# Layer B, one core: sums, values, inverses and scalings of two halves issued apart, filling in smaller pieces, inverse totals on Pool

## The chip, the cores and the metric

The kernel runs on 1 core of one Trainium2 chip. The metric is the device time of one execution in microseconds (us). A core has five engines that run their own instruction streams and wait for one another through semaphores: PE (matrix multiply; its weight loads are listed apart as PEld), DVE (vector), ACT (scalar), POOL (GpSimd) and SP, which issues DMA. In the timelines below, the work of an engine runs in the order in which the program issues it to that engine (the KT copy at 1005.63 us comes after the multiply at 1005.22, as issued), so what stands ahead of an instruction on its engine is part of its cost.

## The reference, cut to what matters

The model is four layers, A, B, A, B. Only B is changed. B walks through 2048 tokens in 64 segments of 32. Each segment is joined to 8 memory rows, and the first 8 output rows are the memory of the next segment, so the segments are serial.

```python
for s in range(n_seg):                              # 64 steps
    xs = x[:, s * seg_len:(s + 1) * seg_len, :].copy()
    h = jnp.concatenate([mem, xs], axis=1)          # 8 + 32 rows
    q = jnp.einsum('btd,dhe->bhte', h, Wq)          # 32 heads of 128; k and v alike
    ...
    scores = jnp.where(mask[None, None], scores, -1000000000.0)
    p = _softmax(scores, axis=-1)
    o = jnp.einsum('bhqk,bhke->bhqe', p, v)
    o = jnp.einsum('bhte,hed->btd', o, Wo)
    mem = o[:, :M, :].copy()                        # the next step waits for this
    outs.append(o[:, M:, :])
```

## The kernel before

The 32 heads are worked on as two halves, b = 0 and 1. For a half, `scores(b)` makes the logits and ACT their exponentials (PT). PE then makes the softmax sums (a matrix of ones times PT) and the values (V times PT) into a PSUM buffer pair, `OTL[b, 0]` and `OTL[b, 1]`. ACT makes the inverses R of the sums as exp(-ln(sum)), and DVE multiplies the values by R into OTsb, which the output passes (OPS) read. There are only two OTL buffers: those of half 1 are those of half 0 again, free when DVE's multiplies of half 0 are done. The multiplies and inverses are named (b, jp) below: (0,1) is the second quarter. The other names: QT and KT are queries and keys, transposed for the scores, and TPQ and TPK are PE's transposes that they are copied from; msb is a step's output in bf16, MT its memory rows transposed, hT the next step's input; tsb and ttp are results of the filling and their transposes. `ln_norm` is the layernorm of later tokens, and one of its operations, pow, runs on Pool.

```python
            def sums_and_values(b):
                for jp in range(2):
                    OTL[b, jp] = pot.tile([128, 2, 2, 256], F32, name="b_OTL", tag="ot")   # 2 buffers
                ...  # 8 matmuls of sums, then 32 of values

            def normalize(b, jp):
                R = (wk if general else sm).tile([128, 2, 160], F32, name="b_R", tag="R")   # 2 buffers
                o = OTL[b, jp]
                nc.scalar.activation(out=R[:], in_=o[:, :, 1, 0:160], func=ACT.Ln)
                acc = {} if general else {"accum_out": seen[:, 2 + 2 * b + jp:3 + 2 * b + jp]}
                nc.scalar.activation(out=R[:], in_=R[:], func=ACT.Exp, scale=-1.0, **acc)
                h = 16 * b + 8 * jp
                nc.vector.tensor_tensor(out=OTsb[:, h:h + 8, :]..., in0=o[:, :, 0, 0:160], in1=R[:], op=ALU.mult)
            ...
            if not general:
                sums_and_values(0)
                normalize(0, 0)
            TPKb = transp4(Ksb[:, 1, :], "b_TPK")
            scatter("dve", TPKb, 1, heads(KT[s]), 0, 8, 24)       # KT: the second scores need it
            ...
            scores(1)
            normalize(0, 1)
            for f in vparts[3:]:
                f()
            evac("dve", Vsb[:, 1, :], Vb[:])                      # Vsb: the second values need it
            fill(0.9)
            sums_and_values(1)
            normalize(1, 0)
            normalize(1, 1)
            op = OPass(lambda h: OTsb[:, h, 0:32], HORDER, "b_OPS")
            op.run(8)
            fill(0.7 if i4 else 0.9)
            op.run(8)
            ops = op.ps
            fill(0.4)
            ...      # msb (ACT), MT (PE), hT (DVE and ACT): the memory of the next step
```

`fill` gives PE independent work where it would wait. With i4 the number of the step modulo 4, in three of four steps it is ten parts of four matmuls (b_tail), in the fourth (i4 = 0) sixteen parts of a deferred output pass (b_OPSd). `general` is False on the path that runs. The totals of sums and inverses (`seen`, `C.tot`) only feed a range check at the end.

Of the kernel before, what the change touches and what calls it, by code (L numbers as in the profile page):

```python
# [18 lines left out]
F32 = mybir.dt.float32  # L19
BF16 = mybir.dt.bfloat16  # L20
ACT = mybir.ActivationFunctionType
ALU = mybir.AluOpType
AX = mybir.AxisListType
# [6 lines left out]
NCH = 5  # L30
# [549 lines left out]
def layer_B(nc, tc, C, W, wo_src, x_src, xb_src, x_dst, mem0, general, nsteps=64, out_bf16=False):  # L580
# [8 lines left out]
    nc = _OrdNC(tc, nc_raw, engines=ORDER_ENGINES)  # L589
    assert nsteps % 4 == 0  # L590
    NT = nsteps // 4
    with ExitStack() as ctx:
        st = ctx.enter_context(tc.tile_pool(name="b_state", bufs=1))
        wk2 = ctx.enter_context(tc.tile_pool(name="b_wk2", bufs=2))
        hp = qkp = sm = wk2
        wk = st
# [10 lines left out]
        nc.vector.tensor_tensor(out=selm[:, 1, :], in0=C.identb[:, 56:64], in1=C.identb[:, 120:128], op=ALU.add)  # L607
        ones = st.tile([128, 128], BF16, name="b_ones")
        nc.vector.memset(ones[:], 1.0)
        XO = st.tile([64, 320], F32, name="b_XO")  # L610
        nc.vector.memset(XO[:], 0.0)
        negs = wk.tile([128, 32], F32, name="b_negs", tag="Qsb")
# [64 lines left out]
        hT, QT, KT = {}, {}, {}  # L677

        def heads(t):
            return t[:, 0:1280].rearrange("p (h c) -> p h c", c=40)  # L680
# [36 lines left out]
        def scatter(eng, tp, b, dst3, t0, t1, c0):  # L717
            src = tp[:].rearrange("p i (j t) -> p i j t", j=4)[:, :, :, t0:t1]
            dst = dst3[:, 16 * b:16 * b + 16, c0:c0 + (t1 - t0)].rearrange("p (j i) c -> p i j c", j=4)
            evac(eng, dst, src)  # L720
# [83 lines left out]

        def add_out(ops, XO, name):

            nc.vector.tensor_tensor(out=XO[0:64, :], in0=ops[0:64, :], in1=XO[0:64, :], op=ALU.add)
            if out_bf16:
                xnb = wk.tile([64, 320], BF16, name=name, tag=name)
                nc.vector.tensor_tensor(out=xnb[0:64, :], in0=ops[64:128, :], in1=XO[0:64, :], op=ALU.add)  # L810
                return xnb
# [19 lines left out]
        for kind in ("Q", "K", "V"):  # L831
            for b in range(2):
                u = TailUnit(0, kind, b, ("act", "dve")[b])
# [23 lines left out]
        for s in range(nsteps):  # L857
            last = (s == nsteps - 1)
            T, i4 = divmod(s, 4)
# [8 lines left out]
            if i4 == 0:  # L868
                units = [deferred.pop(T - 1)] if T >= 1 else []
            elif T + 1 < NT:  # L870
                kind = " VQK"[i4]
                units = [TailUnit(T + 1, kind, 0, "act"), TailUnit(T + 1, kind, 1, "dve")]
            else:
                units = []
            queue = [(0.22, u) for u in units for _ in range(NCH)] if i4 else [(0.15, u) for u in units for _ in range(16)]

            def fill(us):

                while queue and us > 0.05:
                    cost, u = queue.pop(0)  # L880
                    u.run(1)
                    us -= cost

            cols = lambda c: hT[s][:, c, 24:56]
# [4 lines left out]
            PT = wk.tile([128, 2, 2, 4, 40], BF16, name="b_PT", tag="PT")  # L889
            OTsb = wk.tile([128, 32, 40], BF16, name="b_OTsb", tag="OTsb")  # L890
            OTL = {}
            if not general:
                seen = sm.tile([128, 6], F32, name="b_seen", tag="seen")
            mrows = []

            def row_max(b):

                negm = wk.tile([128, 16], F32, name="b_negm", tag="negm")
                for q in range(2):
                    sp = ps_tile([40, 8, 40], F32, "b_Sq")  # L900
                    nc.tensor.matmul(sp[:], lhsT=C.identb[:, 0:40], rhs=maskq[:].unsqueeze(1).to_broadcast([128, 8, 40]),
                                     start=True, stop=False, skip_group_check=True)
                    for i in range(8):
                        h = 16 * b + 8 * q + i
                        nc.tensor.matmul(sp[:, i, :], lhsT=QT[s][:, 40 * h:40 * h + 40], rhs=KT[s][:, 40 * h:40 * h + 40],
                                         start=False, stop=True, skip_group_check=True)
                    nc.vector.tensor_reduce(out=negm[0:40, 8 * q:8 * q + 8], in_=sp[:], axis=AX.X, op=ALU.max, negate=True)
                parts = wk.tile([128, 3, 16], BF16, name="b_mparts", tag="mparts")
                for i in range(3):
                    nc.vector.tensor_copy(parts[0:40, i, :], negm[0:40, :])  # L910
                    if i < 2:
                        nc.vector.tensor_tensor(out=negm[0:40, :], in0=negm[0:40, :], in1=parts[0:40, i, :], op=ALU.subtract)
                tp = ps_tile([48, 40], BF16, "b_mt")
                nc.tensor.transpose(tp[:], parts[0:40].rearrange("p i h -> p (i h)"), C.identb[0:40, 0:40])
                ms = wk.tile([48, 40], BF16, name="b_ms", tag="ms")
                nc.vector.tensor_copy(ms[:], tp[:])
                mr = wk.tile([3, 16, 40], BF16, name="b_mrows", tag="mrows")
                for i in range(3):
                    nc_raw.sync.dma_start(mr[i:i + 1, :, :], ms[16 * i:16 * i + 16, :])
                mrows.append(mr)  # L920
# [18 lines left out]
                acc = {} if general else {"accum_out": seen[:, b:b + 1]}  # L939
                nc.scalar.activation(out=PT[:, b], in_=sp[:], func=ACT.Exp, **acc)  # L940

            def sums_and_values(b):

                for jp in range(2):
                    OTL[b, jp] = pot.tile([128, 2, 2, 256], F32, name="b_OTL", tag="ot")
                def ot(j):
                    return OTL[b, j // 2][:, j % 2]
                for k, n in ((0, 32), (1, 8)):
                    for j in range(4):
                        nc.tensor.matmul(ot(j)[:, 1, 0:160], lhsT=ones[32 * j:32 * j + n, :], rhs=PT[32 * j:32 * j + n, b, k].rearrange("p r c -> p (r c)"),  # L950
                                         start=(k == 0), stop=(k == 1), tile_position=(32 * j, 0))
                for r in range(4):
                    for k, n in ((0, 32), (1, 8)):
                        V_ = Vsb if k == 0 else Vt[s]
                        for j in range(4):
                            nc.tensor.matmul(ot(j)[:, 0, 40 * r:40 * r + 40], lhsT=V_[32 * j:32 * j + n, b, 128 * r:128 * r + 128],
                                             rhs=PT[32 * j:32 * j + n, b, k, r, :], start=(k == 0), stop=(k == 1), tile_position=(32 * j, 0))

            def normalize(b, jp):
                R = (wk if general else sm).tile([128, 2, 160], F32, name="b_R", tag="R")  # L960
                o = OTL[b, jp]
                nc.scalar.activation(out=R[:], in_=o[:, :, 1, 0:160], func=ACT.Ln)
                acc = {} if general else {"accum_out": seen[:, 2 + 2 * b + jp:3 + 2 * b + jp]}
                nc.scalar.activation(out=R[:], in_=R[:], func=ACT.Exp, scale=-1.0, **acc)
                h = 16 * b + 8 * jp
                nc.vector.tensor_tensor(out=OTsb[:, h:h + 8, :].rearrange("p (j r) c -> p j (r c)", j=2), in0=o[:, :, 0, 0:160], in1=R[:], op=ALU.mult)

            Qa = thin_mm(cols, W.wq, 0, "b_Qa")
            evac("act", Qsb[:, 0, :], Qa[:], SCB)
# [23 lines left out]
            TPQb = transp4(Qsb[:, 1, :], "b_TPQ")  # L993
            scatter("act", TPQb, 1, heads(QT[s]), 0, 8, 24)
            if not last:
                scatter("act", TPQb, 1, heads(QT[s + 1]), 8, 32, 0)
            if not general:
                sums_and_values(0)
                normalize(0, 0)
            TPKb = transp4(Ksb[:, 1, :], "b_TPK")  # L1000
            scatter("dve", TPKb, 1, heads(KT[s]), 0, 8, 24)
            if not last:
# [4 lines left out]
            if general:  # L1007
                row_max(0)
                scores(0)
                sums_and_values(0)  # L1010
                normalize(0, 0)
                row_max(1)
            scores(1)
            normalize(0, 1)
            for f in vparts[3:]:
                f()
            evac("dve", Vsb[:, 1, :], Vb[:])
            fill(0.9)
            sums_and_values(1)
            normalize(1, 0)  # L1020
            normalize(1, 1)
            op = OPass(lambda h: OTsb[:, h, 0:32], HORDER, "b_OPS")
            op.run(8)
            fill(0.7 if i4 else 0.9)
            op.run(8)
            ops = op.ps
            fill(0.4)
            if not general:
                nc.gpsimd.tensor_tensor(out=C.tot[:, 0, 0:2], in0=C.tot[:, 0, 0:2], in1=seen[:, 0:2], op=ALU.add)
                nc.gpsimd.tensor_tensor(out=C.tot[:, 1, 0:4], in0=C.tot[:, 1, 0:4], in1=seen[:, 2:6], op=ALU.add)  # L1030
            g_need = (s + 6) // 4
            if s % 4 == 2 and g_need < NT:
                ln_norm(g_need)
# [11 lines left out]
            if not last:  # L1045
# [9 lines left out]
                fill(9)  # L1055
                if i4 != 3:
                    tails_to_seg(s + 1)
            for u in units:
                if isinstance(u, TailUnit):
                    u.transposes()  # L1060
                    u.finish()
            if not last and i4 == 3:
                tails_to_seg(s + 1)
            if s % 4 == 1 and (s + 7) // 4 < NT:
# [16 lines left out]
            if last:  # L1081
                od = deferred.pop(T)
                od.run(100)
                store_deferred(T, od)
            hT.pop(s); QT.pop(s); KT.pop(s); Vt.pop(s)


def full_kernel(tc, A_x, A_wq, A_wk, A_wv, A_wo, A_beta, B_x, B_mem0, B_Wq, B_Wk, B_Wv, B_Wo, B_seg_len, out, layers="ABAB"):
# [89 lines left out]
```

## Time and profile before

| | before |
|---|---|
| time, median of 3 runs | 3167.43 us (3160.98 to 3169.33) |
| the 128 steps of layer B, from the trace | about 2,370 us of a span of 3,160 us |
| one step, by its place in a group of four | 17.77, 19.07, 19.46, 17.77 us |

Four successive steps, i4 = 1, 2, 3 and 0, in the table of stretches (start and end in us, length, then per engine busy us and number of instructions, granted PE clock as a share of full speed, DMA share, GB/s):

```profile
996.34:1014.11 17.77, 15.98 (x392) 8.46 (x393) 6.82 (x16) 8.80 (x27) 3.48 (x12) 1.00 0.10 23
1014.11:1033.18 19.07, 16.63 (x400) 8.87 (x400) 8.74 (x21) 9.46 (x28) 2.54 (x8) 1.00 0.06 12
1033.18:1052.64 19.46, 16.88 (x407) 9.01 (x405) 7.01 (x16) 9.98 (x28) 1.13 (x4) 1.00 0.09 21
1052.64:1070.41 17.77, 15.96 (x418) 9.08 (x417) 6.32 (x15) 8.27 (x25) 1.52 (x6) 1.00 0.06 15
```

PE is the busiest and no other engine is busy for more than 52% of a step. PE's waits are then what can be won. This is the view of who waited for whom, PE alone, over the whole run (waiter and its instruction, what it waited for: total us, times, longest us):

```profile
PE b_OTL L86 <- DVE b_OTsb L86: 87.7, 128, 1.2
PE b_SP L86 <- DVE b_KT L86: 78.0, 128, 0.9
PE b_ttp L86 <- DVE b_tsb L86: 37.6, 64, 0.9
PE b_OTL L86 <- DVE b_Vsb L86: 36.3, 128, 0.3
...
PE b_OPS L86 <- DVE b_OTsb L86: 18.5, 93, 0.5
```

The same in order of time, in the timeline of one step (start, length, engine, operation, output<-inputs, count, and in brackets the idle time before it and what ended it):

```profile
1005.22 0.49 DVE L86 TENSOR_TENSOR b_OTsb<-b_OTL,b_R 128x320 bf16<-128x320 f32 x1 [1.31 <-ACT b_R L86]
1005.63 0.48 DVE L86 COPY b_KT<-b_TPK 128x128 bf16<-128x128 bf16 x2
1005.90 0.38 PE L86 MATMUL b_SP<-b_QT,b_KT 128*32 128x40 bf16 x32 [0.53 <-DVE b_KT L86]
...
1006.38 0.44 ACT L86 ACTIVATE b_PT<-b_SP 128x320 bf16<-128x320 f32 x1 [1.25 <-PE b_SP L86]
...
1006.81 0.43 ACT L86 ACTIVATE b_R<-b_OTL 128x320 f32<-128x320 f32 x1
...
1007.87 0.49 DVE L86 TENSOR_TENSOR b_OTsb<-b_OTL,b_R 128x320 bf16<-128x320 f32 x1 [1.76 <-ACT b_R L86]
1008.28 0.68 DVE L86 CAST b_Vsb<-b_V 128x512 bf16<-128x512 f32 x1
1008.42 0.31 PE L86 MATMUL b_OTL<-b_PT,b_ones 32*128 32x160 bf16 x6 [0.64 <-DVE b_OTsb L86]
...
1009.32 1.27 PE L86 MATMUL b_OPS<-b_wo,b_OTsb 128*32 128x320 bf16 x32
1009.48 0.44 ACT L86 ACTIVATE b_R<-b_OTL 128x320 f32<-128x320 f32 x1 [1.64 <-PE b_OTL L86]
```

One reads it from PE backwards. The second sums (1008.42) wait for the multiply that starts at 1007.87; that one waits for the inverse whose Ln (1006.81) ACT runs behind the second PT (1006.38); PT waits for the scores; and the scores (1005.90) wait for a copy that DVE runs behind another multiply (1005.22). It is a zigzag through three engines, none of them full.

The prediction also rests on two groups of Pool additions, for their cost by size (busy us, mean ns):

```profile
L86 POOL TENSOR_TENSOR a_Onat<-a_ts 128x320 bf16<-128x320 f32 x48 | 49.1, 1023 | 11.7 <-DVE a_ts L86 11.7
...
L86 POOL TENSOR_TENSOR c_tot<-c_tot,a_r 128x16 f32<-128x16 f32 x64 | 14.0, 219 | 3.9 <-DVE a_r L86 3.9
```

### The profile page before, as it was taken

To read this page: it belongs to the slowest core of one execution; us is meant where nothing else is said; L and a number is where in the kernel's file an instruction comes from. 1 tells how busy PE (TensorE), PEld (TensorE's weight loads), DVE (VectorE), ACT (ScalarE), POOL (GpSimd) and SP (SyncE) were. 2 spreads that over 40 slices of the span, in tenths; PEclk is the share of its full clock that TensorE was granted. 3 is DMA by queue.
4 is the path that set the end of the run, shared out by engine and by line. 5 is a ranking of instruction groups with operands and counts; after the bars stand their busy time and mean duration, and the time that the engine had idled before them with its cause. 6 is when DMAs were issued, how large, how long until landed. Compare 5 with 4: busy or idle time off the path is not lost.

```text
span 3160.3 us, 128983 instructions
## 1 busy us (share of the span) xinstructions
PE 2698.3 (85%) x57568; PEld 1443.2 (46%) x57568; DVE 1359.2 (43%) x3279; ACT 1580.0 (50%) x3953; POOL 530.0 (17%) x1569
## 2 busy tenths in 40 slices
PE   6888788888888888888778886888888888888887
PEld 3444344444444444444434443444444444444443
DVE  4666333333333343333356662333343343333332
ACT  4666344444454445444456672454444544454443
POOL 2344211111111111111123441111111111111110
PEclk9999799999999999999978996999999999999998
DMA  6332300000000000000123333000000000000000
GB/s 254 128 95 91 107 15 18 19 18 18 18 18 17 18 17 18 18 16 16 37 70 113 109 93 111 14 16 15 16 16 15 15 15 16 17 15 15 14 13 11
DMA packets 98150, 132.19 MB, mean 42 GB/s; under 512 B 19872, under 2 KB 83376, under 8 KB 95664
## 3 DMA queue, kind: packets, MB, share of 16 engines
q1 hardware_dynamic: 95984, 122.19, 13.4%
q8 instruction: 452, 7.41, 1.0%
q10 hardware_dynamic: 1600, 1.66, 0.2%
q14 instruction: 114, 0.93, 0.1%
HBM read 89.17 MB, written 26.21 MB: 37 GB/s over the span
## 4 chain that ended last, share of the span: by engine, by line
PE 48%; ACT 20%; DVE 16%; issue 6%; DMA 2%; POOL 1%; SPq 0%; DVEq 0%; ACTq 0%; POOLq 0%
ACT b_R L86 11%; DVE b_OTsb L86 6%; PE b_Qa L86 5%; PE b_V L86 5%; PE b_Kb L86 5%; PE b_Ka L86 4%; PE b_Qb L86 4%; PE b_SP L86 4%; PE b_OPS L86 3%; ACT b_QT L86 3%; DVE b_Vsb L86 2%; PE a_PP L86 2%; PE b_TPQ L86 2%; ACT b_PT L86 2%; PE b_OTL L86 2%
## 5 line engine op out<-in xcount | busy, mean ns | idle before, releaser
L86 DVE TENSOR_TENSOR b_OTsb<-b_OTL,b_R 128x320 bf16<-128x320 f32 x512 | 251.8, 492 | 669.5 <-ACT b_R L86 669.5
L86 PEld LDWEIGHTS <-b_hT 128*32 128x32 bf16 x15520 | 393.7, 96 | 318.4 <-issue 29.3
L86 PE MATMUL b_OPS<-b_wo,b_OTsb 128*32 128x320 bf16 x8192 | 357.5, 308 | 20.5 <-DVE b_OTsb L86 18.5
L86 ACT ACTIVATE a_PT<-a_S 128x768 bf16<-128x768 f32 (+1 forms) x384 | 326.0, 893 | 80.5 <-PE a_S L86 71.8
L86 POOL TENSOR_TENSOR c_tot<-c_tot,b_seen 128x2 f32<-128x2 f32 (+1 forms) x256 | 50.5, 197 | 1871.4 <-ACT b_PT L86 1306.1
L86 PE MATMUL b_V<-b_wv,b_hT 128*32 128x512 bf16 x5120 | 348.4, 382 | 0.0
L86 ACT ACTIVATE b_R<-b_OTL 128x320 f32<-128x320 f32 x512 | 223.7, 437 | 211.0 <-PE b_OTL L86 211.0
L86 PEld LDWEIGHTS <-b_OTsb 128*32 128x32 bf16 x8192 | 191.6, 98 | 143.7 <-DVE b_OTsb L86 94.6
L86 ACT ACTIVATE b_R<-b_R 128x320 f32<-128x320 f32 x512 | 241.5, 472 | 16.3
L86 DVE CAST b_Ksb<-b_Kb 128x512 bf16<-128x512 f32 x128 | 88.5, 692 | 304.2 <-PE b_Kb L86 304.2
L86 ACT COPY b_QT<-b_TPQ 128x128 bf16<-128x128 bf16 x508 | 164.5, 379 | 84.2 <-PE b_TPQ L86 84.2
L86 ACT ACTIVATE b_PT<-b_SP 128x320 bf16<-128x320 f32 x256 | 112.2, 438 | 161.5 <-PE b_SP L86 158.6
L86 PE MATMUL b_OTL<-b_PT,b_ones 32*128 32x160 bf16 (+1 forms) x2048 | 111.8, 235 | 89.5 <-DVE b_OTsb L86 87.7
L86 ACT ACTIVATE b_Qsb<-b_Qb 128x512 bf16<-128x512 f32 x128 | 76.6, 598 | 200.2 <-PE b_Qb L86 200.2
L86 DVE COPY b_KT<-b_TPK 128x128 bf16<-128x128 bf16 x508 | 122.8, 283 | 119.8 <-PE b_TPK L86 119.8
L86 PE MATMUL b_Qa<-b_wq,b_hT 128*32 128x512 bf16 x2560 | 164.6, 386 | 6.8 <-DVE b_hT L86 2.2
L86 ACT ACTIVATE b_Qsb<-b_Qa 128x512 bf16<-128x512 f32 x128 | 76.6, 598 | 177.6 <-PE b_Qa L86 175.8
L86 PE MATMUL b_Ka<-b_wk,b_hT 128*32 128x512 bf16 x2560 | 164.3, 385 | 0.0
L86 PE MATMUL b_SP<-b_QT,b_KT 128*32 128x40 bf16 (+1 forms) x8192 | 96.9, 181 | 78.0 <-DVE b_KT L86 78.0
L86 PE MATMUL b_Kb<-b_wk,b_hT 128*32 128x512 bf16 x2560 | 163.3, 380 | 0.0
L86 PE MATMUL b_Qb<-b_wq,b_hT 128*32 128x512 bf16 x2560 | 162.3, 381 | 0.0
L86 PE MATMUL a_PP<-a_xnT,a_wt 128*128 128x512 bf16 x560 | 155.1, 412 | 2.3 <-DVE a_t1k L86 0.9
(177 smaller groups left out, 4388.0 us busy)
## 6 DMA issues: line engine op xcount, KB each, us to landing
a_wt<-a_wpad SPq DMA_DIRECT2D x112, 160.0 KB
b_wo<-in_B_Wo_dram SPq DMA_DIRECT2D x8, 1280.0 KB
b_Vt<-b_Vtb SPq DMA_DIRECT2D x512, 16.0 KB
b_XO<-xres SPq DMA_DIRECT2D x256, 30.0 KB
a_wvo<-in_A_wo_dram SPq DMA_DIRECT2D x8, 800.0 KB
b_wq<-in_B_Wq_dram SPq DMA_DIRECT2D x5, 1024.0 KB
b_wk<-in_B_Wk_dram SPq DMA_DIRECT2D x5, 1024.0 KB
b_wv<-in_B_Wv_dram SPq DMA_DIRECT2D x5, 1024.0 KB
```

The lines of the kernel that those rows point to most:

```text
L86: r = f(*a, **k)
```

## The change

The intent, as the diff shows it: take the two scalings out of the way of the KT copies, start both inverses of half 0 early, break the filling into finer pieces at more places, and take the totals of the inverses off ACT. The core of it:

```diff
-            queue = [(0.22, u) for u in units for _ in range(NCH)] if i4 else [(0.15, u) for u in units for _ in range(16)]
+            queue = []      # parts as before, then, for Q and K, the tail's transposes as an item of 0.31
...
-                while queue and us > 0.05:
+                while queue and us > 0.1:
...
-            def normalize(b, jp):
+            def inverse(b, jp):
+                R = Rs[b, jp] = (wk if general else sm).tile([128, 2, 160], F32, name="b_R", tag="R")
+                nc.scalar.activation(out=R[:], in_=OTL[b, jp][:, :, 1, 0:160], func=ACT.Ln)
+                nc.scalar.activation(out=R[:], in_=R[:], func=ACT.Exp, scale=-1.0)
+
+            def scale(b, jp):
+                R = Rs.pop((b, jp))
                 h = 16 * b + 8 * jp
+                nc.vector.tensor_tensor(out=OTsb[:, h:h + 8, :]..., in0=OTL[b, jp][:, :, 0, 0:160], in1=R[:], op=ALU.mult)
+                if not general:
+                    for i in range(2):
+                        nc.gpsimd.tensor_tensor(out=Rtot[:], in0=Rtot[:], in1=R[:, i], op=ALU.add)
...
-                scatter("act", TPQb, 1, heads(QT[s + 1]), 8, 32, 0)
+                scatter("dve", TPQb, 1, heads(QT[s + 1]), 8, 32, 0)
             if not general:
-                sums_and_values(0)
-                normalize(0, 0)
+                sums(0)
+                values(0)
+                inverse(0, 0)
+                inverse(0, 1)
             ...                                   # KT copies
+                scale(0, 0)
             scores(1)
-            normalize(0, 1)
             for f in vparts[3:]:
                 f()
             evac("dve", Vsb[:, 1, :], Vb[:])
-            fill(0.9)
-            sums_and_values(1)
-            normalize(1, 0)
-            normalize(1, 1)
+            scale(0, 1)
+            fill(0.66)
+            sums(1)
+            fill(0.22)
+            values(1)
             op = OPass(lambda h: OTsb[:, h, 0:32], HORDER, "b_OPS")
             op.run(8)
-            fill(0.7 if i4 else 0.9)
-            op.run(8)
+            for jp in range(2):
+                inverse(1, jp)
+                scale(1, jp)
+            op.run(4)
+            fill(0.33)
+            op.run(4)
             ops = op.ps
-            fill(0.4)
+            fill(0.6)
```

In parts of filling per step (of ten): before 4 ahead of the sums, 3 between the halves of the output passes, 2 after them, 1 after MT; changed 3 ahead of the sums, 1 between sums and values, 2 ahead of the last quarter of the output passes, 3 after them, 1 after MT.

More of the change, by code (lines that the diff above doesn't have):

```diff
@@ L609, in layer_B @@
         nc.vector.memset(ones[:], 1.0)
+        if not general:
+            Rtot = st.tile([128, 160], BF16, name="b_Rtot")
+            nc.vector.memset(Rtot[:], 0.0)
         XO = st.tile([64, 320], F32, name="b_XO")
@@ L874, in layer_B @@
                 units = []
-            queue = [(0.22, u) for u in units for _ in range(NCH)] if i4 else [(0.15, u) for u in units for _ in range(16)]
+            queue = []
+            for u in units:
+                if isinstance(u, TailUnit):
+                    queue += [(0.22, lambda u=u: u.run(1))] * NCH
+                else:
+                    queue += [(0.15, lambda u=u: u.run(1))] * 16
+            for u in units:
+                if isinstance(u, TailUnit) and u.kind != "V":
+                    queue.append((0.31, lambda u=u: (u.transposes(), u.finish())))
             def fill(us):
-                while queue and us > 0.05:
-                    cost, u = queue.pop(0)
-                    u.run(1)
+                while queue and us > 0.1:
+                    cost, f = queue.pop(0)
+                    f()
                     us -= cost
@@ L892, in layer_B @@
             if not general:
-                seen = sm.tile([128, 6], F32, name="b_seen", tag="seen")
+                seen = sm.tile([128, 2], F32, name="b_seen", tag="seen")
             mrows = []
@@ L940, in scores, with ot, sums, values @@
                 nc.scalar.activation(out=PT[:, b], in_=sp[:], func=ACT.Exp, **acc)
-            def sums_and_values(b):
+            def ot(b, j):
+                return OTL[b, j // 2][:, j % 2]
+            def sums(b):
                 for jp in range(2):
                     OTL[b, jp] = pot.tile([128, 2, 2, 256], F32, name="b_OTL", tag="ot")
-                def ot(j):
-                    return OTL[b, j // 2][:, j % 2]
                 for k, n in ((0, 32), (1, 8)):
                     for j in range(4):
-                        nc.tensor.matmul(ot(j)[:, 1, 0:160], lhsT=ones[32 * j:32 * j + n, :], rhs=PT[32 * j:32 * j + n, b, k].rearrange("p r c -> p (r c)"),
+                        nc.tensor.matmul(ot(b, j)[:, 1, 0:160], lhsT=ones[32 * j:32 * j + n, :], rhs=PT[32 * j:32 * j + n, b, k].rearrange("p r c -> p (r c)"),
                                          start=(k == 0), stop=(k == 1), tile_position=(32 * j, 0))
+            def values(b):
                 for r in range(4):
@@ L955, in sums_and_values @@
                         for j in range(4):
-                            nc.tensor.matmul(ot(j)[:, 0, 40 * r:40 * r + 40], lhsT=V_[32 * j:32 * j + n, b, 128 * r:128 * r + 128],
+                            nc.tensor.matmul(ot(b, j)[:, 0, 40 * r:40 * r + 40], lhsT=V_[32 * j:32 * j + n, b, 128 * r:128 * r + 128],
                                              rhs=PT[32 * j:32 * j + n, b, k, r, :], start=(k == 0), stop=(k == 1), tile_position=(32 * j, 0))
-            def normalize(b, jp):
-                R = (wk if general else sm).tile([128, 2, 160], F32, name="b_R", tag="R")
-                o = OTL[b, jp]
-                nc.scalar.activation(out=R[:], in_=o[:, :, 1, 0:160], func=ACT.Ln)
-                acc = {} if general else {"accum_out": seen[:, 2 + 2 * b + jp:3 + 2 * b + jp]}
-                nc.scalar.activation(out=R[:], in_=R[:], func=ACT.Exp, scale=-1.0, **acc)
+            Rs = {}
+            def inverse(b, jp):
[4 more added lines that the diff above has]
+                R = Rs.pop((b, jp))
                 h = 16 * b + 8 * jp
-                nc.vector.tensor_tensor(out=OTsb[:, h:h + 8, :].rearrange("p (j r) c -> p j (r c)", j=2), in0=o[:, :, 0, 0:160], in1=R[:], op=ALU.mult)
+                nc.vector.tensor_tensor(out=OTsb[:, h:h + 8, :].rearrange("p (j r) c -> p j (r c)", j=2), in0=OTL[b, jp][:, :, 0, 0:160], in1=R[:], op=ALU.mult)
+                if not general:
+                    for i in range(2):
+                        nc.gpsimd.tensor_tensor(out=Rtot[:], in0=Rtot[:], in1=R[:, i], op=ALU.add)
             Qa = thin_mm(cols, W.wq, 0, "b_Qa")
@@ L1009, in layer_B @@
                 scores(0)
-                sums_and_values(0)
-                normalize(0, 0)
+                sums(0)
+                values(0)
+                inverse(0, 0)
+                scale(0, 0)
+                inverse(0, 1)
                 row_max(1)
+            else:
+                scale(0, 0)
             scores(1)
-            normalize(0, 1)
             for f in vparts[3:]:
@@ L1017, in layer_B @@
             evac("dve", Vsb[:, 1, :], Vb[:])
-            fill(0.9)
-            sums_and_values(1)
-            normalize(1, 0)
-            normalize(1, 1)
+            scale(0, 1)
[3 more added lines that the diff above has]
+            values(1)
             op = OPass(lambda h: OTsb[:, h, 0:32], HORDER, "b_OPS")
             op.run(8)
-            fill(0.7 if i4 else 0.9)
-            op.run(8)
+            for jp in range(2):
[4 more added lines that the diff above has]
+            op.run(4)
             ops = op.ps
-            fill(0.4)
+            fill(0.6)
             if not general:
-                nc.gpsimd.tensor_tensor(out=C.tot[:, 0, 0:2], in0=C.tot[:, 0, 0:2], in1=seen[:, 0:2], op=ALU.add)
-                nc.gpsimd.tensor_tensor(out=C.tot[:, 1, 0:4], in0=C.tot[:, 1, 0:4], in1=seen[:, 2:6], op=ALU.add)
+                nc.gpsimd.tensor_tensor(out=C.tot[:, 0, 0:2], in0=C.tot[:, 0, 0:2], in1=seen[:], op=ALU.add)
             g_need = (s + 6) // 4
@@ L1057, in layer_B @@
                     tails_to_seg(s + 1)
-            for u in units:
-                if isinstance(u, TailUnit):
-                    u.transposes()
-                    u.finish()
             if not last and i4 == 3:
@@ L1085, in layer_B @@
             hT.pop(s); QT.pop(s); KT.pop(s); Vt.pop(s)
+        if not general:
+            rt = sm.tile([128, 1], F32, name="b_rt", tag="seen")
+            nc.vector.tensor_reduce(out=rt[:], in_=Rtot[:], axis=AX.X, op=ALU.add)
+            nc.vector.tensor_tensor(out=C.tot[:, 1, 0:1], in0=C.tot[:, 1, 0:1], in1=rt[:], op=ALU.add)
 def full_kernel(tc, A_x, A_wq, A_wk, A_wv, A_wo, A_beta, B_x, B_mem0, B_Wq, B_Wk, B_Wv, B_Wo, B_seg_len, out, layers="ABAB"):
```

## The prediction

> **What bounds it now.** The timeline shows 128 steps of layer B (2 layers x 64) repeating in fours of 17.77, 19.07, 19.46 and 17.77 us (74.07): 2,370 of 3,160 us. Layer A is untouched. A window table gives per step PE busy 16 to 17 us, DVE about 7, ACT about 9, clock 1.00: a chain zigzagging PE, ACT, DVE paces it. In the step from 996.34 the timeline shows PE idle at: second scores, 0.53 us, behind the KT copy, which DVE issues after the first OTsb multiply; second sums, 0.64, for the OTL buffer freed by multiply (0,1), whose Ln and Exp ACT runs after the second PT exp; second values, 0.28, behind the Vsb cast queued after that multiply; output passes, 0.2 to 0.5, for OTsb; then the msb and hT copies.
>
> **What changes, per step.**
> 1. One of four QT copies goes from ACT (379 ns) to DVE (283 ns).
> 2. Both inverses of half 0 precede the second PT exp; the KT copies precede the first multiply. Second scores lose their wait: 0.6 us earlier (0.9 where layernorm transposes delay ACT).
> 3. The Vsb cast precedes multiply (0,1): values no longer wait for it. The buffer's release moves from 1008.36 to about 1007.28; 12 instead of 16 filling matmuls precede the sums, 4 follow.
> 4. Four Exp lose their accumulate reads (190 ns, 90 overlapped): multiplies of half 1 come 0.1 us earlier each.
> 5. Half 1: 48 output matmuls, 8 filling, 16, 12 filling. A wait of about 0.7 us for OTsb(1,0) appears, since filling was moved away from it; that for OTsb(1,1) is covered.
> 6. Pool gets eight 128x160 additions. From 219 ns at 16 columns and 1,023 at 320 I estimate 600 ns each, 5 us per step, on an engine busy 2 us. The Trainium skill, "GPSIMD Engine Reference", section 3.1, has about 2.6 cycles an element for a two-input addition; this trace's slope (2.64 ns) is nearer 3.2 at its 1.2 GHz. Pool stays off the chain, except in the 19.07 us step, where the layernorm's pow queues behind the additions.
> 7. The queued transposes leave PE's order as it was.
>
> Trace durations laid end to end (estimate): values start at 1007.66 instead of 1009.02, output passes at 1007.96 instead of 1009.32, msb at 1011.31 instead of 1012.80, next step 1.5 us earlier. Gains: 1.5, 1.4 (Pool-limited), 1.8, 1.5: about 6.2 of 74.07 us, times 32: 198 us. All lies on the chain, since steps are serial through hT. I take off a little for waits not seen.
>
> **Predicted: 2985 us, 8 in 10 between 2935 and 3055. Chances: faster by over 2% 0.94, within 2% 0.05, slower 0.01.**
>
> **What would show it.** Steps near 16.3, 17.6, 17.6, 16.3 us. PE's wait for KT before second scores near 0 (now 78 us in all); OTL's wait for Vsb gone; OTL's wait for OTsb about 0.5 us per step still there; a wait of 0.6 to 0.7 us for OTsb at the output passes. No accumulate reads on R. Rtot additions near 600 ns, Pool busy about 530 + 600 us.
>
> **What would make it wrong.** Pool additions of 900 ns or more: the 19.07 us steps gain almost nothing (about 40 us lost); above some 1.3 us they also hold the two R buffers and delay the inverses of half 1. Denser PE lowering the granted clock (1.00 in B, about 0.9 in A). Multiply (0,1), being behind the Vsb cast, releasing OTL later than I think: then about 1 us per step, near 3,050.

## The result, and the profile after

The changed kernel takes 3001.65 us (median of 4 runs, 3000.38 to 3005.86), the kernel before in the same rounds 3164.58 us. The ratio is 0.9487, with a 95% interval of 0.9468 to 0.9505.

The four steps, which are now 16.70, 17.81, 18.04 and 16.69 us:

```profile
954.99:971.69 16.70, 15.84 (x402) 8.35 (x390) 6.95 (x17) 8.08 (x21) 6.83 (x19) 1.00 0.11 24
971.69:989.50 17.81, 16.50 (x400) 8.95 (x400) 9.13 (x22) 8.79 (x23) 6.52 (x17) 1.00 0.06 13
989.50:1007.54 18.04, 16.75 (x407) 9.07 (x405) 7.37 (x17) 9.21 (x23) 4.76 (x11) 1.00 0.09 23
1007.54:1024.23 16.69, 15.76 (x419) 8.91 (x420) 7.11 (x17) 7.55 (x20) 5.21 (x13) 1.00 0.08 16
```

They lose 74.07 - 69.24 = 4.83 us per four steps, times 32 is 155 us of the 162 that the profiled span lost. Nothing but layer B's steps has to be looked at. PE's waits after:

```profile
PE b_OPS L86 <- DVE b_OTsb L86: 58.6, 128, 0.5
PE b_OTL L86 <- DVE b_OTsb L86: 52.4, 128, 0.7
PE b_ttp L86 <- DVE b_tsb L86: 32.2, 64, 0.9
```

The waits for KT and Vsb are gone, that for the OTL buffer is smaller, and that at the output passes has tripled. The timeline of the step that corresponds to the one shown above:

```profile
963.03 0.49 DVE L86 COPY b_KT<-b_TPK 128x128 bf16<-128x128 bf16 x2 [0.20 <-PE b_TPK L86]
...
963.80 0.49 DVE L86 TENSOR_TENSOR b_OTsb<-b_OTL,b_R 128x320 bf16<-128x320 f32 x1 [0.27 <-ACT b_R L86]
...
963.93 0.38 PE L86 MATMUL b_SP<-b_QT,b_KT 128*32 128x40 bf16 x32
...
964.82 0.69 DVE L86 CAST b_Vsb<-b_V 128x512 bf16<-128x512 f32 x1 [0.53 <-PE b_V L86]
...
965.42 0.48 DVE L86 TENSOR_TENSOR b_OTsb<-b_OTL,b_R 128x320 bf16<-128x320 f32 x1
965.96 0.31 PE L86 MATMUL b_OTL<-b_PT,b_ones 32*128 32x160 bf16 x6 [0.36 <-DVE b_OTsb L86]
966.20 0.40 PE L86 MATMUL b_tail<-b_wv,b_hx 128*32 128x512 bf16 x4
966.84 1.27 PE L86 MATMUL b_OPS<-b_wo,b_OTsb 128*32 128x320 bf16 x32
...
967.05 0.44 ACT L86 ACTIVATE b_R<-b_OTL 128x320 f32<-128x320 f32 x1 [2.10 <-POOL b_Rtot L86]
...
968.57 0.73 PE L86 MATMUL b_OPS<-b_wo,b_OTsb 128*32 128x320 bf16 x16 [0.46 <-DVE b_OTsb L86]
```

Two things in it are to be tested. A single part of filling (966.20) stands between the sums and the values, while the values' operand, Vsb, has long been cast. And the Ln at 967.05 is said to wait 2.10 us for Pool. The chain that ended last says the same, by engine:

```profile
PE 61%; DVE 9%; ACT 8%; issue 7%; POOL 6%; DMA 1%; SPq 0%; POOLq 0%; DVEq 0%; ACTq 0%
```

The new group of additions, in the list of groups (busy us, mean ns, idle time of Pool before them):

```profile
L86 POOL TENSOR_TENSOR b_Rtot<-b_Rtot,b_R 128x160 bf16<-128x160 bf16 x1024 | 502.9, 491 | 1347.8 <-ACT b_R L86 1287.6
```

Because nearly all steps with the same i4 repeat to about 0.01 us, they can be laid over each other. This table gives, for the steps with i4 = 1 (the 17.77 us of the first line above), the median time in us from the first matmul of the step. It is worked out from the traces, and all experiments are read with it:

| event | before | after | old filling (a3) | release first (b1) | c1 |
|---|---|---|---|---|---|
| second scores begin (first matmul after the mask's) | 9.56 | 8.94 | 8.95 | 8.94 | 8.95 |
| multiply (0,1) done, OTL free | 12.02 | 10.91 | 10.92 | 10.06 | 10.07 |
| Vsb cast done | 12.62 | 10.52 | 10.53 | 10.65 | 10.66 |
| values begin | 12.67 | 11.55 | 11.07 | 10.95 | 10.72 |
| Ln (1,0) begins | 13.14 | 12.06 | 11.63 | 11.46 | 11.24 |
| third quarter of output passes begins | 14.75 | 13.58 | 13.19 | 12.98 | 12.77 |
| last quarter begins | 15.68 | 14.57 | 13.98 | 13.96 | 13.58 |
| MT begins | 16.94 | 15.86 | 15.24 | 15.26 | 14.84 |
| next step begins | 17.77 | 16.70 | 16.07 | 16.10 | 15.68 |

### The profile page after: what moved, and what is told of

Its sections match the earlier page's. It is cut to its first block, busy times and chain, and to the rows that moved or that the text cites. A ratio compares the mean times of both kernels' runs of the same rounds, so it can differ in the third digit from the quotient of the medians.

```text
span 2998.1 us, 129696 instructions
## 1 busy us (share of the span) xinstructions
PE 2659.2 (89%) x57506; PEld 1431.5 (48%) x57568; DVE 1408.6 (47%) x3411; ACT 1487.9 (50%) x3315; POOL 998.8 (33%) x2465
## 4 chain that ended last, share of the span: by engine, by line
PE 61%; DVE 9%; ACT 8%; issue 7%; POOL 6%; DMA 1%; SPq 0%; POOLq 0%; DVEq 0%; ACTq 0%
PE b_V L86 10%; PE b_Qa L86 5%; PE b_Kb L86 5%; PE b_Ka L86 5%; POOL b_Rtot L86 5%; ACT b_R L86 5%; PE b_Qb L86 5%; PE b_SP L86 5%; PE b_OPS L86 4%; PE b_tail L86 4%; PE b_TPQ L86 3%; PE a_PP L86 2%; PE b_TPK L86 2%; DVE b_OTsb L86 2%; PE b_OTL L86 2%
## 5 line engine op out<-in xcount | busy, mean ns | idle before, releaser
L86 POOL TENSOR_TENSOR b_Rtot<-b_Rtot,b_R 128x160 bf16<-128x160 bf16 x1024 | 502.9, 491 | 1347.8 <-ACT b_R L86 1287.6
L86 PE MATMUL b_OPS<-b_wo,b_OTsb 128*32 128x320 bf16 x8192 | 347.8, 301 | 59.4 <-DVE b_OTsb L86 58.6
L86 POOL TENSOR_SCALAR_AFFINE_SELECT a_PT<-a_PT 128x256 bf16<-128x256 bf16 x256 | 109.8, 433 | 212.3 <-ACT a_PT L86 197.7
L86 PE MATMUL b_OTL<-b_PT,b_ones 32*128 32x160 bf16 (+1 forms) x2048 | 111.6, 234 | 54.2 <-DVE b_OTsb L86 52.4
L86 ACT COPY b_QT<-b_TPQ 128x128 bf16<-128x128 bf16 (+1 forms) x382 | 115.7, 340 | 84.4 <-PE b_TPQ L86 84.4
L86 PE MATMUL a_PP<-a_xnT,a_wt 128*128 128x512 bf16 x505 | 148.5, 408 | 9.2 <-issue 5.5
L86 PE MATMUL a_S<-a_qk 32*128 32x512 bf16 (+3 forms) x1024 | 143.2, 321 | 7.1 <-ACT a_PT L86 5.8
```

Source lines behind the costliest of these rows:

```text
L86: r = f(*a, **k)
```

## The experiments

My theory after the result: the issue order of half 0 gives the gain; the new places of the filling give part of it back; Pool is hidden. The rivals: each part of the change contributes; or Pool, with its 6% of the chain, now limits half 1.

| run | median us | ratio to before | 95% interval |
|---|---|---|---|
| changed kernel | 3001.65 | 0.9487 | 0.9468 to 0.9505 |
| a1_acc_on_act | 3009.62 | 0.9511 | 0.9496 to 0.9527 |
| a2_order_only | 2947.21 | 0.9314 | 0.9299 to 0.9330 |
| a3_old_filling | 2934.53 | 0.9274 | 0.9259 to 0.9290 |
| a4_no_inverse_totals | 2988.83 | 0.9445 | 0.9430 to 0.9461 |
| b1_release_first | 2923.85 | 0.9250 | 0.9234 to 0.9265 |
| b2_fill_at_wait | 2951.65 | 0.9337 | 0.9321 to 0.9352 |
| b4_pool_twice | 3143.10 | 0.9949 | 0.9932 to 0.9966 |
| c1_release_first_old_filling | 2889.26 | 0.9145 | 0.9130 to 0.9160 |
| c2_all_three | 2848.96 | 0.8998 | 0.8983 to 0.9013 |
| c3_all_three_spread | 2833.44 | 0.8953 | 0.8938 to 0.8968 |

Each has 4 runs, all correct. The runs of the kernel before that they share had medians of 3165.34 us (a1 to a4), 3160.93 (b1 to c1) and 3165.20 (c2, c3).

### a1_acc_on_act: the totals back on ACT

```diff
-                nc.scalar.activation(out=R[:], in_=R[:], func=ACT.Exp, scale=-1.0)
+                nc.scalar.activation(out=R[:], in_=R[:], func=ACT.Exp, scale=-1.0, **acc)
...
-                        nc.gpsimd.tensor_tensor(out=Rtot[:], in0=Rtot[:], in1=R[:, i], op=ALU.add)
```

> The changed kernel with one part undone: the inverse totals are again accumulated by ACT in the second Exp, and Pool does no additions. My theory: Pool is off the chain although the chain of waits gives it 6% (the R buffer is released at 9.9 us of the step, the Ln that reuses it starts at 12.06, 0.5 us after the values, as it did before the change). The accumulate reads lengthen half 1 by 0.1 us for each of its two Exp: steps 0.1 to 0.2 us longer, 13 to 25 us in all, so 3015 to 3027 us. Rival (the chain of waits taken at its word: ACT waits 236 us for Pool before the Ln): without Pool's additions the time falls by 50 us or more.

Measured: 3009.62 us, 8 us slower than the changed kernel; I had expected 13 to 25. The 95% intervals of the two ratios overlap, so the 8 us rest on the traces: the steps are 0.04 to 0.13 us longer. The rival, a fall of 50 us or more, is ruled out. The reads cost what was expected at the output passes (multiply (1,1) starts 0.13 us later), but a small gain that I had not counted comes against it, which a4 explains.

### a4_no_inverse_totals: on neither engine

```diff
-                if not general:
-                    for i in range(2):
-                        nc.gpsimd.tensor_tensor(out=Rtot[:], in0=Rtot[:], in1=R[:, i], op=ALU.add)
```

> The changed kernel without any totals of the inverses (they only feed a range check, the output stays right), on neither engine: the floor for that part. My theory: same as the changed kernel within 5 us (2997 to 3003 us), since Pool's additions are hidden, also in the steps with the layernorm, where its pow could start at 15.66 by the vector engine alone and starts at 15.67. Rival (Pool on the chain for 5 to 6% by the chain of waits): faster by 50 us or more; my prediction's Pool limit in one step of four: faster by 3 us at most.

Measured: 2988.83 us, 13 us faster than the changed kernel, where I had expected 5 at most. Every step is 0.05 us shorter (128 x 0.05 = 6.4 us), and the B layers together are 8 us shorter from their first steps to their last (2170.1 against 2178.3 us in the profiled runs); the rest lies outside B and is not settled. The 0.05 us is not Pool's work. The R buffer that Ln (1,0) takes is free at 9.91 us of the step, when Pool's second addition ends, and Ln begins at 12.06. But in the changed kernel Ln starts 0.51 us after the values began, and here 0.46. The instruction records show where it arises. In the changed kernel this Ln itself waits for Pool, long done, and its wait for the values stands in a separate semaphore instruction ahead of it (ACT has 1,033 of these instead of 873); that one ends when the values are done, and Ln starts 0.045 us after it. In this run Ln itself waits for the values; a separate instruction, a wait for DVE, stands ahead of it here too, but it ended 2.56 us before Ln started. The Trainium skill, "Perfetto Trace Analysis", section "Identifying Dependency Chains", says that an instruction that waits for several engines may have separate semaphore instructions put ahead of it. This trace agrees, and shows a cost of about 0.05 us where the wait that ends last stands in the separate instruction. So "2.10 <-POOL b_Rtot" is a wait for the values, put down to Pool.

In the steps with the layernorm, its pow on Pool starts at 15.62 us instead of 15.67, no more than the multiply (1,1) ahead of it has moved. In the changed kernel Pool's last addition ends at 15.36 us, 0.31 us before pow. The vector engine sets that time, not Pool.

### a2_order_only and a3_old_filling: the new order with the filling of before

```diff
             scale(0, 1)
-            fill(0.66)
+            fill(0.9)
             sums(1)
-            fill(0.22)
             values(1)
             ...
             op.run(8)
-            op.run(4)
-            fill(0.33)
-            op.run(4)
+            fill(0.7 if i4 else 0.9)
+            op.run(8)
             ops = op.ps
-            fill(0.6)
+            fill(0.4)
```

a3 is the changed kernel with this edit; a2 has in addition the totals on ACT. Both also have the old threshold of `fill` (0.05) and the old place of the inverses of half 1 in the program. Both keep the queued transposes; PE's order of work at the end of the steps that have them is the same before and after in the traces.

> Only the issue order of half 0 is changed (inverses of both quarters ahead of the second scores, KT copies ahead of the multiplies, one QT copy on DVE, Vsb cast ahead of the second multiply); totals on ACT and filling amounts and places as in the kernel before. My theory: the new order gives all of the gain and more; values start about 1.45 us earlier than before: steps near 16.3 to 16.4 us instead of 16.70, 2945 to 2975 us. Rival (each part of the change contributes to the gain): slower than the changed kernel, 3020 to 3080 us.

> The changed kernel with the filling amounts and places of the kernel before (4 parts ahead of the sums, none between sums and values, 3 between the two halves of the output passes, 2 after them). My theory: the four filling matmuls between sums and values lie on the chain with all of their time plus the two switches of operand shape, 0.4 us; without them values start 0.2 us after the buffer's release: steps near 16.15 us, 2925 to 2955 us. Rival (the smaller pieces of filling cover waits better): slower, 3020 us or more.

Measured: 2947.21 and 2934.53 us, both where my theory had them and far from the rivals' 3020 and more. The order alone is 6.9% faster than before; Pool's totals take another 0.4 points; the new filling gives 2.1 points back (0.9487 against 0.9274). The table of events shows where: the buffer is free at the same time in both (10.91 and 10.92 us), and the values begin at 11.55 or at 11.07. What each exchange within the order gives is not separated, except for that of the cast and the multiply (b1).

### b2_fill_at_wait: one part moved

```diff
             sums(1)
-            fill(0.22)
             values(1)
             ...
+            fill(0.22)
             op.run(4)
             fill(0.33)
```

> The changed kernel with one part of filling (four matmuls) moved from between sums and values to ahead of the third quarter of the output passes, where PE waits 0.46 us. My theory: values start at 11.07 instead of 11.55 us of the step, as with the old filling, and the wait at the output passes hides the moved part: steps near 16.25 us, 2935 to 2955 us. If the loss of the new filling lay in the output passes or after them instead: no gain, or under 15 us.

Measured: 2951.65 us, as expected: 50 us for moving four matmuls per step. The values begin at 11.06 us, and PE's wait for OTsb at the output passes falls from 58.6 to 32.5 us in all. The instruction records of one step show what the four cost between sums and values. The last sum starts at 11.054 us, the four start together at 11.213 and take 389 ns each, and the first value starts at 11.545: 0.49 us, where four of a long run of such matmuls take 0.22 (20 of them take 1.08 us). The sums and values are tiled by rows (32*128 in the listing), the filling by columns (128*32). The Trainium skill, "TensorEngine Tiling (Array Packing)", section "Tiling Modes", says that a change of the tiling mode drains the engine. The trace fits this, though it does not show a drain as such: with both changes, the four cost 0.27 us more than in a long run. A rival is that any short run of filling costs more. In c3 below, the same four stand between two groups of output passes, which are tiled as they are. There the filling starts 0.125 us after the last output matmul, which is the pitch of the output matmuls themselves, and the next group 0.27 us later: an excess of 0.05 us, part of which may be a wait. So about 0.22 us go with the changed tiling.

### b1_release_first: one exchange on DVE

The kernel before had the multiply (0,1) ahead of the Vsb cast. The change turned the two round, and this run turns them back.

```diff
-            evac("dve", Vsb[:, 1, :], Vb[:])
             scale(0, 1)
+            evac("dve", Vsb[:, 1, :], Vb[:])
             fill(0.66)
```

> The changed kernel with one exchange on the vector engine: the second multiply of half 0, which frees the sums and values buffer, is issued ahead of the cast of the second values' operand instead of behind it. My theory (the second half waits for that buffer at 10.92 us of the step; R is there at 9.55): release at about 10.07, the cast done at 10.68, the sums follow the filling at 10.37 without a wait, values at about 10.97 instead of 11.55; steps near 16.1 us, 2915 to 2940 us. Rival (half 1 is limited by Pool's hold on R, as the chain of waits says): no change, within 10 us of the changed kernel's 3000.

Measured: 2923.85 us, 78 us faster than the changed kernel by one exchanged line. So this part of the change was a loss: with the inverses early, the multiply is ready before the cast. The release moves from 10.91 to 10.06 us and the cast only from 10.52 to 10.65. PE's wait for the buffer is gone (first line of b1's list, and the one that was 52.4 us):

```profile
PE b_OPS L86 <- DVE b_OTsb L86: 58.4, 128, 0.5
...
PE b_OTL L86 <- DVE b_OTsb L86: 0.4, 2, 0.2
```

That Pool's additions stay as they are, and half 1 still moves as a whole by 0.6 us, is a second disproof of the rival.

### b4_pool_twice: how much slack Pool has

```diff
-                    for i in range(2):
+                    for i in (0, 1, 0, 1):
                         nc.gpsimd.tensor_tensor(out=Rtot[:], in0=Rtot[:], in1=R[:, i], op=ALU.add)
```

> The changed kernel with every Pool addition of inverses done twice (16 a step at about 0.57 us; the total is doubled, the range check still passes). It measures Pool's slack. My theory: single additions are off the chain; doubled, those of (0,1) end at 13.4 us of the step and hold the R buffer 0.5 us past the time its Ln wants it (12.92), and the layernorm's pow moves from 15.67 to about 18.2 in one step of four. Steps of 17.1 us, and 20 us instead of 17.82: 3090 to 3140 us. If Pool is on the chain already (its 6% in the chain of waits): each of the 503 us that it adds counts, 3300 us or more.

Measured: 3143.10 us, 3 us above the range that my theory gave and far below the rival's. Some 500 us of added Pool work cost 141 us. Two kinds of steps came as expected: 17.0 to 17.2 us, with Ln (1,1) held to 13.34, and 20.12 us with pow at 17.97. The step after the layernorm's did not: of 30, 16 took 20.0 to 20.3 us, two 19.5 and 19.6, and 12 about 18.3. PE waited about 2.48 us for the second transposes just before the 18 slow ones, but also before ten of the twelve others. In the slow ones, its matmuls then ran at half speed. The timeline of PE in a slow one, and the table of stretches over the same time:

```profile
733.81 0.40 PE L86 MATMUL b_ttp<-c_identb,b_tsb 128*128 128x128 bf16 x4 [2.48 <-DVE b_tsb L86]
734.14 1.77 PE L86 MATMUL b_Qa<-b_wq,b_hT 128*32 128x512 bf16 x20
735.68 2.36 PE L86 MATMUL b_Ka<-b_wk,b_hT 128*32 128x512 bf16 x20
```

```profile
731.00:734.14 3.14, 0.66 (x11) 0.39 (x10) 1.18 (x3) 0.75 (x2) 3.04 (x9) 1.00 0.00 0
734.14:736.50 2.36, 2.36 (x30) 0.99 (x32) 1.31 (x3) 0.50 (x1) 0.00 (x0) 0.63 0.02 7
736.50:738.50 2.00, 2.00 (x28) 0.85 (x24) 0.42 (x1) 0.10 (x1) 0.00 (x0) 0.58 0.16 42
738.50:742.00 3.50, 3.50 (x89) 1.76 (x85) 0.76 (x3) 2.07 (x6) 0.00 (x0) 1.00 0.06 13
```

The granted clock (the number ahead of the last two) falls: by the clock records of the trace it is 0.5 from 734.75 to 738.16 us, for 3.41 us, and the 0.63 and 0.58 of the table are means with full speed. Each of the 18 slow steps has one such record of 0.5 for 3.41 us, none of the twelve others has. The slow steps are longer than 18.35 us by about 1.7 us in 16 and 1.2 in two, so some 30 of the 141 us (an estimate from these lengths) are the clock's. That is more than the 3 us by which I missed.

### c1_release_first_old_filling

The exchange of b1 and the filling of a3, with 3 parts ahead of the sums instead of 4.

```diff
-            evac("dve", Vsb[:, 1, :], Vb[:])
             scale(0, 1)
+            evac("dve", Vsb[:, 1, :], Vb[:])
             fill(0.66)
             sums(1)
-            fill(0.22)
             values(1)
             ...      # then as a3
```

> The exchange of b1 together with the filling places of the kernel before, with three parts ahead of the sums instead of four. My theory: values start when the cast of their operand is done, at 10.73 us of the step instead of 11.07 with the old filling alone; all after it moves with it: steps of about 15.75, 15.75, 17.05 and 17.1 us, 2880 to 2910 us.

Measured: 2889.26 us, as expected. Values begin at 10.72 us, right after the cast.

### c2_all_three and c3_all_three_spread: the steps with transposes

In two of four steps PE makes transposes after MT, and it waits there for a cast on DVE (32.2 us in all in the changed kernel). c2 takes that cast ahead of the hT copies and issues the layernorm's work early; no run separates these two edits. c3 moves one part into a wait that was left.

```diff
+            g_need = (s + 6) // 4                 # after the first KT copies, was near the step's end
+            if s % 4 == 2 and g_need < NT:
+                ln_norm(g_need)
...
             ops = op.ps
-            fill(0.4)
+            fill(0.9 if i4 >= 2 else 0.4)         # c2: all ten parts ahead of MT
```

```diff
-            fill(0.7 if i4 else 0.9)
-            op.run(8)
+            fill(0.7)
+            op.run(4)
+            fill(0.15)                            # c3: one part between the last two quarters
+            op.run(4)
             ops = op.ps
-            fill(0.9 if i4 >= 2 else 0.4)
+            fill(0.66 if i4 >= 2 else 0.4)
```

> c1 and, in the two steps of four that make transposes (16.98 and 17.23 us there), all ten parts of filling ahead of the hidden-state matmuls, so that the last cast is done when the transposes want it; and the layernorm's statistics issued early in the step, in the vector engine's idle time after the first KT copies. My theory: the vector engine's chain at the step's end (layernorm apply until 15.90, cast, second transposes at 16.65) sets these steps; steps of about 15.7, 15.7, 16.4 and 16.6 us, 2835 to 2870 us. Rival: the extra filling delays the hidden-state matmuls by what it saves, 2880 us or more.

> c2 with one of the ten parts moved into the 0.38 us that PE waits between the third and the last quarter of the output passes. My theory: that wait hides it, the last cast comes 0.2 us sooner; steps of 15.7, 15.7, 16.2 and 16.45 us, 2820 to 2860 us. Rival: the two switches of operand shape make the part cost more than the wait, slower than c2.

Measured: 2848.96 and 2833.44 us. c3 beats both kernels: 10.5% faster than before (ratio 0.8953), where the change was 5.1%. Its four steps:

```profile
913.18:928.86 15.68, 15.52 (x396) 8.36 (x393) 7.20 (x17) 8.02 (x22) 6.62 (x18) 1.00 0.11 26
928.86:944.96 16.10, 15.91 (x401) 8.72 (x402) 9.17 (x22) 8.18 (x23) 6.52 (x18) 1.00 0.07 15
944.96:961.29 16.33, 16.14 (x407) 8.84 (x405) 7.28 (x17) 8.99 (x24) 4.80 (x12) 1.00 0.10 25
961.29:976.97 15.68, 15.55 (x418) 8.81 (x417) 6.95 (x17) 7.87 (x21) 5.20 (x13) 1.00 0.08 18
```

PE is now busy for 63.13 of 63.79 us, so little more is to be had by order alone. (A busy PE is not PE at its peak.)

## Why the prediction was right, and where it was off

It said 2985 us, 2935 to 3055; it was 3001.65. The direction, the range and the chain of waits were right: half 0's order sets when half 1 can start. But it laid the change end to end as a whole and did not ask which parts gain. Two did not: the new filling, and the cast ahead of the multiply. Point by point:

- **"Second scores lose their wait: 0.6 us earlier."** Right: the first of them starts at 8.94 instead of 9.56 us of the step, and PE's wait for KT, 78.0 us, is gone.
- **"The buffer's release moves from 1008.36 to about 1007.28."** Right: 12.02 to 10.91 us of the step, 1.11 us against 1.08.
- **"Values start at 1007.66 instead of 1009.02."** The term that failed most. The gain is 12.67 - 11.55 = 1.12 us, not 1.36. I had in effect given the rest of the sums and the four filling matmuls 0.32 us, by their rate in a long run; between two row-tiled groups they took 0.58 (10.97 to 11.55). b2 shows the whole effect: without them values begin at 11.06.
- **"A wait of about 0.7 us for OTsb(1,0) appears."** Right in kind, 0.46 us per step (58.6/128) in size. The wait for OTsb(1,1) is covered, as predicted.
- **"OTL's wait for OTsb about 0.5 us per step still there."** 0.41 (52.4/128). What I did not see: that this wait is free to take away. The cast was issued ahead of the multiply although it waits for PE, while R had been ready since 9.54 us; b1 gains 78 us with that. Point 3 counted this order as part of the gain, because the values no longer wait for the cast; but the sums then wait for the multiply behind it.
- **"Multiplies of half 1 come 0.1 us earlier each"** by the accumulate reads. Right for the reads (a1: multiply (1,1) 0.13 us later with them), but the wait for the values in a separate semaphore instruction ahead of Ln takes 0.05 us back, which I had not counted. The net gain of moving the totals is 8 us.
- **"I estimate 600 ns each"** for Pool's additions. They took 491 ns. An estimate from the rate in the Trainium skill, "GPSIMD Engine Reference", section 3.1, 2.6 cycles an element at 1.2 GHz, is 347 ns for 160 without a fixed cost, and 16 columns take 219 ns; the measurement decides.
- **"Pool stays off the chain, except in the 19.07 us step."** Right for the rule, wrong for the exception: pow waits for the vector engine (a4). That step gained 1.25 us, not 1.4.
- **"Gains: 1.5, 1.4, 1.8, 1.5: about 6.2 of 74.07 us."** 1.07, 1.25, 1.42 and 1.08, together 4.8. In the step that the prediction laid out (i4 = 1), 0.24 of the missing 0.43 us is lost before the values begin and about 0.14 from there to msb. Moving the four filling matmuls to a wait (b2) brings this step to 16.26 us, a gain of 1.51. In addition, in the steps with i4 = 0, 20 filling matmuls come after MT, where the kernel before had 4, and the next step begins 1.09 us after MT; it is 0.84 where i4 = 1, and in a3, which again has 4.
- **The 16 us taken off for waits not seen** brought the number near by luck: they stood for no cause that was then found. What I did not ask is whether the new filling was a gain at all. By a2 and a3 it costs 2.1 points of what the order had won.

## What to carry to other kernels

When a serial chain runs through several engines, write down for each engine what stands ahead of the instruction that frees a buffer, and issue the one whose inputs are ready first: one exchanged pair of vector instructions was worth 78 us here. Put filling where PE waits anyway and not between two groups on the chain, above all when it is tiled another way: four matmuls that take 0.22 us in a run cost 0.49 us there. A profile's name for the engine that ended a wait is a hint to be tested; here it named Pool for 236 us of waits, and without any Pool additions the time fell by 13.

## What the Trainium skill lacked or had wrong

- "TensorEngine Tiling (Array Packing)", section "Tiling Modes": says that a change of the tiling mode drains the engine, with no figure. Here two changes around four concurrent 128x512 matmuls cost 0.27 us more than the matmuls' share of a long run (0.49 against 0.22 us). Of this, about 0.22 us go with the tiling: between groups of the same tiling (c3) the excess is at most 0.05.
- "Perfetto Trace Analysis", section "Identifying Dependency Chains": names the extra semaphore instructions, with no cost. Here about 0.05 us where the wait that ends last stands in the extra instruction, and nothing that shows where it was met 2.56 us earlier (a4).
- "TensorE: Matmul & The Clock Gate", Part 1, table of the two states, gives an idle window of about 3.4 us for the fall to half clock, and its section "Why this matters for your kernels" warns of idle gaps above about 3 us. Here each of the 18 slow steps of b4 has a granted clock of 0.5 for 3.41 us, which agrees with the half clock and with the length of the window. The gap before it was 2.48 us of idle PE, or about 3.1 us (3.3 in two of them) if the transposes on either side are counted as idle. Neither reaches 3.4 us, but the ends of matmuls are modelled in these traces, and no run tells which of the two counts. The page does not say how often a gap of this length leads to half clock: it was followed by half clock in 18 of 28 steps. That some were and some were not fits the free-running window that the page describes.
- "GPSIMD Engine Reference", section 3.1, gives cycles per element of a two-input addition, but no fixed cost in ns for a small one: 219 ns at 16 columns of f32, 491 ns at 160 columns in bf16 with an f32 operand, 1,023 ns at 320 columns of f32 here.
